# Transposing softmax probabilities as 4-byte words in a grouped-query attention kernel

## Chip, core and metric

The kernel runs on one core of a Trainium2 chip. The metric is the device time of one execution in microseconds. A core has TensorE (PE in the profile, with its weight loads as PEld), VectorE (DVE), ScalarE (ACT), GpSimd (POOL) and SyncE (SP), which here issues every DMA.

## What is computed

Two independent problems A and B of the same shape, joined along the last axis. B = 16 batches of 80 query rows of width 576, 32 query heads of width 128, 16 key/value heads (each serves two query heads), and 512 cached keys. All tensors are bf16.

```python
q = (x @ wq).reshape(B, Sq, Hq, Dh).transpose(0, 2, 1, 3)
k = jnp.repeat(k_cache, rep, axis=1); v = jnp.repeat(v_cache, rep, axis=1)
scores = jnp.einsum("bhqd,bhkd->bhqk", q, k) * (Dh ** -0.5)
p = _softmax(scores, axis=-1)
o = jnp.einsum("bhqk,bhkd->bhqd", p, v)
return o.transpose(0, 2, 1, 3).reshape(B, Sq, Hq * Dh) @ wo
```

## The kernel before

The work is cut into four phases (two problems, each in two halves of 8 batches). A phase has four groups of four key/value heads, and a group has eight units, one for each batch: 128 units in all. In a unit, each of the four key/value heads has 160 rows of queries (two heads of 80). They are worked in five tiles of 128 rows by 512 keys: tile k = 0 takes the last 32 rows of all four heads together, tiles k = 1 to 4 the first 128 rows of one head each. That makes 640 tiles.

A tile goes through these steps (line numbers are those of the profile):

- QK on TensorE: one matmul of 512 columns (L436), or for k = 0 four matmuls in 32-column strips of the array (L431), into one of three PSUM banks.
- The row maximum on VectorE (L441), exp with the row sum on ScalarE (L445, into one of ten buffers p_sb of 128 x 512 bf16), for five tiles at a time a reciprocal of the sums on VectorE (L449), and the scaling by it on GpSimd (L452, in place).
- The transposition of P on TensorE (em_tr, L458): four transpositions of 128 x 128 bf16, side by side in one of two PSUM banks. A transposition loads its block of P as weights and streams the identity past it.
- The copy out of PSUM on VectorE (em_ptev, L464 for k = 0 and L466 for the others) into pT.
- P@V on TensorE for k >= 1 (em_pv, L501): four matmuls of 160 columns, V as weights and pT as the streamed operand, added up in PSUM.
- After two heads, the copy of the result into oT on ScalarE (L513).

The keys come by a transposing DMA (L405) that leaves key 4p + j in slot j, column p, and V is loaded the same way (L409), so that column block j of P fits block j of V.

Beside the tiles run the projection of the queries (L335: groups of five matmuls of 480 or 160 columns, scaled out of PSUM by ScalarE at L342 or VectorE at L347) for the group after the present one, the transposition of x (L259), and the output projection (L546: sixteen matmuls of 192 columns, then a copy on ScalarE, L560, or an addition on VectorE, L566, and a store).

The order is written out by hand. Each operation is given an engine and a key (a time in tile steps), and a small planner (_Sched) sorts by key; each engine then runs its list in that order, and semaphores are set where an operation reads or overwrites what another engine made. QK runs eight steps (LA) ahead of the transposition of its tile:

```python
S.add("pe", tq, em_qk, reads=q_reads + [R(("kT", ks), U)],
      writes=[R(("ps", sbk), ("S", T))], name="qk%d" % T)
...
S.add("pe", t0, em_tr, reads=[R(("P", psl), ("n", T)), IDENT],
      writes=[R(("ps", tb), ("T", T))], name="tr%d" % T)
S.add("dve", t0 + KO["ptev"], em_ptev, reads=[R(("ps", tb), ("T", T))], writes=pt_writes,
      name="ptev%d" % T)
```

P@V of a tile has the key t0 + 2.5, so on TensorE the transposition and the QK of later tiles stand between a transposition and the P@V that needs it.

Of the kernel before, what the change touches and what calls it, by code (L numbers as in the profile page):

```python
# [6 lines left out]
BF16 = mybir.dt.bfloat16  # L7
# [127 lines left out]
def bass_concat_heads__gqa_block_cached__gqa_block_cached__near_ridge_kernel(  # L135
# [24 lines left out]
    with ExitStack() as es:  # L160
# [2 lines left out]
        ident = sb("ident", [128, 128], BF16)  # L163
        ones = sb("ones", [128, 128], BF16)
        warm = sb("warm", [128, 512], BF16)
        xs = sb("xs", [128, NRT, D], BF16)
        xT = sb("xT", [128, 2, 5, NROW], BF16)
        wq_sb = sb("wq_sb", [128, 2, 5, 1024], BF16)
# [1 line left out]
        kT = sb("kT", [128, NK, 4, 512], BF16)  # L170
        v_sb = sb("v_sb", [128, NV, 4, 512], BF16)
        p_sb = sb("p_sb", [128, NP, 512], BF16)
        pT = sb("pT", [128, NPT, 4, 4, 160], BF16)
        oT = sb("oT", [128, HQ, NROW], BF16)
        wo_sb = sb("wo_sb", [128, HQ, D], BF16)
        DC = D // NOC
# [4 lines left out]
        rinv = sb("rinv", [128, NSS, 8], F32)  # L181
        ps = es.enter_context(nc.psum_tensor("ps", [128, 8, 512], F32))
        psb = ps[:].bitcast(BF16)

        sem_names = (["e_pe", "e_act", "e_dve", "e_pool", "d_xs", "d_wo0", "d_wo1", "d_wq0", "d_wq1", "d_out0", "d_out1"]
                     + ["d_k%d" % i for i in range(NK)] + ["d_v%d" % i for i in range(NV)])
# [10 lines left out]
        def R(res, ver):  # L197
            return (res, ver)
# [24 lines left out]
        if NWARM:  # L223
            S.add("dve", -1000, em_warmset, writes=[R(("warm",), 0)], name="warmset")
            S.add("pe", -990, em_warm, reads=[R(("ones",), 0), R(("warm",), 0)], writes=[R(("ps", 0), ("W",))],
                  name="warm")
        IDENT = R(("ident",), 0)

        def su_time(goct, bl):
            ph, q = divmod(goct, NOCT)  # L230
# [161 lines left out]
        for U in range(NSU):  # L392
# [23 lines left out]
            for k in range(5):  # L416
# [25 lines left out]
                                           op=AluOpType.max, negate=True)  # L442

                def em_exp(e, sbk=sbk, si=si, psl=psl, ss=ss, col=col):
                    return e.activation(p_sb[:, psl, :], ps[:, sbk, :], AF.Exp, bias=negmax[:, si:si + 1],  # L445
                                        scale=1.0, accum_out=rowsum[:, ss, col:col + 1])

                def em_rcp(e, ss=ss):
# [5 lines left out]

                def em_tr(e, psl=psl, tb=tb):
                    last = None
                    for j in range(4):
                        last = e.transpose(psb[:, tb, j * 128:(j + 1) * 128],  # L458
                                           p_sb[:, psl, j * 128:(j + 1) * 128], ident[:])
                    return last  # L460

                def em_ptev(e, k=k, gl=gl, tb=tb, pts=pts):
                    if k == 0:
                        return e.tensor_copy(pT[:, pts, :, :, 128:160],  # L464
                                             psb[:, tb, 0:512].rearrange("p (j g c) -> p g j c", j=4, g=4))
                    return e.tensor_copy(pT[:, pts, gl, :, 0:128],  # L466
                                         psb[:, tb, 0:512].rearrange("p (j n) -> p j n", j=4))

                if k == 0:
                    q_reads = [R(("qT", qsl, bl, i), goct) for i in (1, 3, 5, 7)]  # L470
# [11 lines left out]
                if col == 4:  # L482
# [2 lines left out]
                S.add("pool", t4 - LA + KO["nrm"] + 0.01 * col, em_nrm,  # L485
                      reads=[R(("ri", ss), G), R(("P", psl), ("e", T))],
                      writes=[R(("P", psl), ("n", T))], name="nrm%d" % T)
                S.add("pe", t0, em_tr, reads=[R(("P", psl), ("n", T)), IDENT],
                      writes=[R(("ps", tb), ("T", T))], name="tr%d" % T)
                S.add("dve", t0 + KO["ptev"], em_ptev, reads=[R(("ps", tb), ("T", T))], writes=pt_writes,  # L490
                      name="ptev%d" % T)
# [1 line left out]
                if k >= 1:  # L493
                    ob = 5 + (gl // 2)
                    off = (gl % 2) * 160
                    pr = gl // 2

                    def em_pv(e, gl=gl, ob=ob, off=off, vs=vs, pts=pts):
                        last = None
                        for j in range(4):  # L500
                            last = e.matmul(ps[:, ob, off:off + 160],  # L501
                                            lhsT=v_sb[:, vs, gl, j * 128:(j + 1) * 128],
                                            rhs=pT[:, pts, gl, j, :], start=(j == 0), stop=(j == 3))
                        return last

                    S.add("pe", t0 + KO["pv"], em_pv,
                          reads=[R(("V", vs), U), R(("pT", pts, gl, "A"), U), R(("pT", pts, gl, "R"), U)],
                          writes=[R(("ps", ob), ("O", U, pr))], name="pv%d.%d" % (U, gl))
                    if gl % 2 == 1:
                        hb = 8 * q + 4 * pr  # L510

                        def em_oev(e, ob=ob, hb=hb, bl=bl):
                            return e.copy(oT[:, hb:hb + 4, bl * SQ:(bl + 1) * SQ],  # L513
                                          ps[:, ob, 0:320].rearrange("p (h s) -> p h s", h=4))

                        S.add("act", t0 + KO["oev"], em_oev, reads=[R(("ps", ob), ("O", U, pr))],
                              writes=[R(("oT", bl, q, pr), ph)], name="oev%d.%d" % (U, pr))

        NB_ = NRT * NOC
        for ph in range(NPH):  # L520
            prob, half = divmod(ph, NPP)
            for hh in range(2):
                for n in range(NB_):
                    r, c3 = divmod(n, NOC)
                    tail = (hh == 1 and ph == NPH - 1)
                    if tail:
                        x = 5.0 * NSU + 4.0 + 1.6 * n
                        bank = (7, 5, 6, 3, 4)[n % 5]
                    else:
                        if hh == 0:  # L530
                            u_a, n_sl = SUPP // 2 + 1, SUPP // 2 - 1
                        else:
                            u_a, n_sl = SUPP + 1, SUPP // 2
                        per = -(-NB_ // n_sl)
                        x = 5.0 * (ph * SUPP + u_a + n // per) + KO["ob"] + 0.35 * (n % per)
                        bank = OBANK
                    t = ftime(x)
                    bls = list(range((128 * r) // SQ, (128 * r + 127) // SQ + 1))
                    pv_ = ("OUT", ph, hh, n)
                    slot = n % 2  # L540

                    def em_op(e, r=r, c3=c3, hh=hh, bank=bank):
                        last = None
                        for hi in range(HH):
                            h = hh * HH + hi
                            last = e.matmul(ps[:, bank, 0:DC], lhsT=oT[:, h, r * 128:(r + 1) * 128],  # L546
                                            rhs=wo_sb[:, h, c3 * DC:(c3 + 1) * DC],
                                            start=(hi == 0), stop=(hi == HH - 1))
                        return last

                    qs_ = [hh * (NOCT // 2) + q_ for q_ in range(NOCT // 2)] if NOCT >= 2 else [0]
                    if NOCT >= 2:
                        ot_reads = [R(("oT", b_, q_, pr_), ph) for b_ in bls for q_ in qs_ for pr_ in range(2)]
                    else:
                        ot_reads = [R(("oT", b_, 0, hh), ph) for b_ in bls]
                    S.add("pe", t, em_op, reads=ot_reads + [R(("wo", hh, wc_), prob) for wc_ in range(NWC)],
                          writes=[R(("ps", bank), pv_)], name="op%d.%d.%d" % (ph, hh, n))
                    if hh == 0:
                        def em_ea(e, r=r, c3=c3, bank=bank):
                            return e.copy(acc[:, r, c3 * DC:(c3 + 1) * DC], ps[:, bank, 0:DC])  # L560

                        S.add("act", t + KO["oeva"], em_ea, reads=[R(("ps", bank), pv_)],
                              writes=[R(("acc", r, c3), ph)], name="oea%d.%d" % (ph, n))
                    else:
                        def em_eb(e, r=r, c3=c3, bank=bank, slot=slot):
                            return e.tensor_tensor(osb[:, slot, :], ps[:, bank, 0:DC],  # L566
                                                   acc[:, r, c3 * DC:(c3 + 1) * DC], AluOpType.add)

                        def em_st(e, r=r, c3=c3, prob=prob, half=half, slot=slot):
                            row0 = half * NROW + 128 * r  # L570
                            dst = out.rearrange("b s d -> (b s) d")[row0:row0 + 128,
                                                                    prob * D + c3 * DC:prob * D + (c3 + 1) * DC]
                            return e.dma_start(dst, osb[:, slot, :])

                        S.add("dve", t + KO["oevb"], em_eb, reads=[R(("ps", bank), pv_), R(("acc", r, c3), ph)],
                              writes=[R(("osb", slot), (ph, n))], name="oeb%d.%d" % (ph, n))
                        S.add("sp", t + KO["oevb"] + KO["ost"], em_st, reads=[R(("osb", slot), (ph, n))],
                              dsem="d_out%d" % slot, name="st%d.%d" % (ph, n))
# [71 lines left out]
```

## Time and profile before

| | |
|---|---|
| median of 3 runs | 815.56 us (814.84 to 816.48) |
| span of the profiled execution, first to last instruction | 812.5 us |
| its granted TensorE clock | 1.00 |
| TensorE instructions | 8940 matmuls, each with a weight load |
| VectorE, ScalarE, GpSimd busy | 680.2, 643.4, 433.0 us |
| DMA | 169.94 MB, mean 209 GB/s |

The profile gives the profiled execution by its span alone; the median of the runs is 3.1 us longer than that span, for what lies before the first and after the last instruction.

In the list of groups, a line shows the source line, the engine, the operation, the tile written and the tiles read, the shapes and the count; then the busy time in us and the mean length of one instruction in ns; then how long the engine was idle just before them and whom it waited for. Matmuls overlap in the array, so the length of one is not the time that it takes from the engine: that is the distance between the starts of two neighbours, which the timeline shows.

### The profile page before, as it was taken

The page shows a single profiled execution, that of the slowest core. Times are in us where ns is not written, and L with a number is a line of the kernel's source. Part 1 is how long each engine was busy: PE and PEld are TensorE (multiplying, and loading weights), DVE is VectorE, ACT ScalarE, POOL GpSimd, SP SyncE. Part 2 cuts the span into 40 slices and gives each one's busy share as a digit, 9 for nine tenths or more (in the row PEclk, how much of TensorE's full clock was granted, in tenths as well). Part 3 has the DMA queues.
Part 4 walks back from the last instruction along what each step waited for, and adds up shares of the span by engine and source line. Part 5 has one row for each costly group of instructions (what it writes and reads, how often), then busy time and mean ns, then how long its engine had stood idle before and what let it go on. Part 6 is the DMA issues. An engine that isn't in the chain of part 4 may idle for free.

```text
span 812.5 us, 23206 instructions
## 1 busy us (share of the span) xinstructions
PE 797.9 (98%) x8940; PEld 620.6 (76%) x8940; DVE 680.2 (84%) x1617; ACT 643.4 (79%) x1725; POOL 433.0 (53%) x647
## 2 busy tenths in 40 slices
PE   7999999999999999999999999999999999999998
PEld 4677678777777777877777777777777778777778
DVE  3899988888888889888888889888888888988872
ACT  2899888888878778888887887888887788888860
POOL 1466665455555546555555555555465455555650
DMA  9999999999897999979789999999978879977601
GB/s 228 243 245 283 249 235 268 260 254 219 190 214 182 224 231 214 207 162 223 180 199 240 245 219 230 237 259 223 224 200 191 200 195 214 199 187 172 156 29 37
DMA packets 363629, 169.94 MB, mean 209 GB/s; under 512 B 278017, under 2 KB 354305, under 8 KB 363521
## 3 DMA queue, kind: packets, MB, share of 16 engines
q1 hardware_dynamic: 363520, 168.46, 90.9%
q8 instruction: 73, 1.20, 0.6%
q14 instruction: 36, 0.29, 0.1%
HBM read 98.37 MB, written 2.95 MB: 125 GB/s over the span
## 4 chain that ended last, share of the span: by engine, by line
PE 90%; DVE 5%; DMA 3%; SPq 0%; issue 0%; POOL 0%; ACT 0%; POOLq 0%
PE ps L335 20%; PE ps L546 19%; PE ps L458 18%; PE ps L501 16%; PE ps L436 12%; PE ps L431 5%; DVE negmax L441 3%; DVE pT L466 1%; DMA kT<-in_A_k_cache_dram 1%; DMA v_sb<-in_A_v_cache_dram 1%; DMA wq_sb<-in_A_wq_dram 1%; PE ps L259 1%; POOL p_sb L452 0%; SPq L292 0%; DVE rinv L449 0%
## 5 line engine op out<-in xcount | busy, mean ns | idle before, releaser
L452 POOL TENSOR_SCALAR p_sb<-p_sb,rinv 128x512 bf16<-128x512 bf16 x640 | 430.5, 695 | 354.6 <-DVE rinv L449 354.6
L445 ACT ACTIVATE p_sb<-ps,negmax 128x512 bf16<-128x512 f32 x640 | 442.3, 691 | 83.4 <-DVE negmax L441 65.3
L441 DVE TENSOR_REDUCE negmax<-ps 128x1 f32<-128x512 f32 x640 | 434.4, 679 | 4.5 <-PE ps L436 2.9
L466 DVE COPY pT<-ps 128x512 bf16<-128x512 bf16 x512 | 209.3, 409 | 93.3 <-PE ps L458 92.6
L458 PE MATMUL ps<-ident,p_sb 128*128 128x128 bf16 x2560 | 248.5, 220 | 4.6 <-DVE negmax L441 3.5
L501 PE MATMUL ps<-pT,v_sb 128*128 128x160 bf16 x2048 | 225.3, 233 | 2.6 <-DMA v_sb<-in_A_v_cache_dram 1.3
L458 PEld LDWEIGHTS ps<-ident,p_sb 128*128 128x128 bf16 x2560 | 175.4, 98 | 57.2 <-DVE qT L347 21.6
L501 PEld LDWEIGHTS ps<-pT,v_sb 128*128 128x128 bf16 x2048 | 169.0, 98 | 63.9 <-DVE qT L347 3.6
L335 PE MATMUL ps<-xT,wq_sb 128*128 128x480 bf16 (+1 forms) x1280 | 214.4, 300 | 1.6 <-DMA wq_sb<-in_A_wq_dram 0.9
L436 PE MATMUL ps<-kT,qT 128*128 128x512 bf16 x512 | 194.0, 379 | 0.0
L546 PE MATMUL ps<-wo_sb,oT 128*128 128x192 bf16 x1920 | 175.7, 246 | 0.0
L546 PEld LDWEIGHTS ps<-wo_sb,oT 128*128 128x128 bf16 x1920 | 158.6, 98 | 0.0
L335 PEld LDWEIGHTS ps<-xT,wq_sb 128*128 128x128 bf16 x1280 | 107.0, 98 | 45.0 <-DVE qT L347 0.9
L513 ACT CAST oT<-ps 128x320 bf16<-128x320 f32 x256 | 108.9, 425 | 35.2 <-PE ps L501 32.9
L445 ACT ACTIVATION_READ_ACCUMULATOR p_sb<-ps,negmax 128x1 f32 x640 | 128.1, 200 | 0.0
L342 ACT ACTIVATE qT<-ps 128x480 bf16<-128x480 f32 (+1 forms) x128 | 71.8, 561 | 25.6 <-PE ps L335 25.5
L464 DVE COPY pT<-ps 128x512 bf16<-128x512 bf16 x128 | 52.9, 413 | 1.3 <-PE ps L458 1.3
L431 PE MATMUL ps<-kT,qT 128*32 128x512 bf16 x512 | 51.2, 390 | 1.4 <-DMA kT<-in_A_k_cache_dram 1.4
L436 PEld LDWEIGHTS ps<-kT,qT 128*128 128x128 bf16 x512 | 50.1, 98 | 0.7
L347 DVE TENSOR_SCALAR qT<-ps 128x160 bf16<-128x160 f32 (+1 forms) x128 | 41.5, 324 | 3.8 <-PE ps L335 3.7
L566 DVE TENSOR_TENSOR osb<-ps,acc 128x192 bf16<-128x192 f32 x60 | 21.0, 349 | 15.3 <-PE ps L546 12.2
L431 PEld LDWEIGHTS ps<-kT,qT 128*32 128x32 bf16 x512 | 13.1, 92 | 14.9 <-DMA kT<-in_A_k_cache_dram 1.6
(16 smaller groups left out, 77.5 us busy)
## 6 DMA issues: line engine op xcount, KB each, us to landing
v_sb<-in_A_v_cache_dram SPq DMA_DIRECT2D x64, 512.0 KB, 4.5
v_sb<-in_B_v_cache_dram SPq DMA_DIRECT2D x64, 512.0 KB, 4.5
wq_sb<-in_A_wq_dram SPq DMA_DIRECT2D x16, 512.0 KB, 5.5
wq_sb<-in_B_wq_dram SPq DMA_DIRECT2D x16, 512.0 KB, 5.5
wo_sb<-in_A_wo_dram SPq DMA_DIRECT2D x8, 576.0 KB, 5.4
wo_sb<-in_B_wo_dram SPq DMA_DIRECT2D x8, 576.0 KB, 4.8
out_dram<-osb SPq DMA_DIRECT2D x60, 48.0 KB, 2.1
xs<-in_A_x_dram SPq DMA_DIRECT2D x2, 720.0 KB, 5.1
```

What stands on the lines that cost most here:

```text
L335: last = e.matmul(ps[:, bank, 0:n1 - n0], lhsT=wq_sb[:, wsl, ck, i * 128:(i + 1) * 128], rhs=xT[:, xsl, ck, n0:n1], start=(ck == 0), stop= ...
L342: return e.activation(qT[:, qsl, b0:b0 + nb, col:col + 80], ps[:, bank, 0:n1 - n0].rearrange("p (b s) -> p b s", b=nb), AF.Identity, scale ...
L431: last = e.matmul(ps[32 * g4:32 * g4 + 32, sbk, :], lhsT=qT[:, qsl, bl, g4 * 160 + 128:g4 * 160 + 160], rhs=kT[:, ks, :, g4 * 128:(g4 + 1) ...
L436: last = e.matmul(ps[:, sbk, :], lhsT=qT[:, qsl, bl, gl * 160:gl * 160 + 128], rhs=kT[:, ks, :, gl * 128:(gl + 1) * 128], start=True, stop ...
L441: return e.tensor_reduce(negmax[:, si:si + 1], ps[:, sbk, :], axis=AX.X, op=AluOpType.max, negate=True)
L445: return e.activation(p_sb[:, psl, :], ps[:, sbk, :], AF.Exp, bias=negmax[:, si:si + 1], scale=1.0, accum_out=rowsum[:, ss, col:col + 1])
L452: return e.tensor_scalar(p_sb[:, psl, :], p_sb[:, psl, :], rinv[:, ss, col:col + 1], 1.0, op0=AluOpType.mult, op1=AluOpType.mult)
L458: last = e.transpose(psb[:, tb, j * 128:(j + 1) * 128], p_sb[:, psl, j * 128:(j + 1) * 128], ident[:])
L466: return e.tensor_copy(pT[:, pts, gl, :, 0:128], psb[:, tb, 0:512].rearrange("p (j n) -> p j n", j=4))
L501: last = e.matmul(ps[:, ob, off:off + 160], lhsT=v_sb[:, vs, gl, j * 128:(j + 1) * 128], rhs=pT[:, pts, gl, j, :], start=(j == 0), stop=(j ...
L513: return e.copy(oT[:, hb:hb + 4, bl * SQ:(bl + 1) * SQ], ps[:, ob, 0:320].rearrange("p (h s) -> p h s", h=4))
L546: last = e.matmul(ps[:, bank, 0:DC], lhsT=oT[:, h, r * 128:(r + 1) * 128], rhs=wo_sb[:, h, c3 * DC:(c3 + 1) * DC], start=(hi == 0), stop=( ...
```

## The change

P's tile is read as 256 words of 4 bytes, and a transposition moves 128 words of 4 bytes a row. Two neighbours in p_sb then travel together. exp writes P so that the two keys of a word are keys i and 128 + i of the same 256-key half: it reads the scores in their old order and writes every second element. The transposed words lie in PSUM as pairs, VectorE copies them as they are (runs of 256 bf16 elements, or 64 for k = 0), and pT holds [half, row, pair]. P@V for key block j reads half j // 2, every second element from j % 2.

The identity for the 4-byte transposition is a copy as 4-byte floats (identf), made by VectorE at the start. A probe, once at the start, transposes the bf16 identity as 4-byte words and sums up every second element of the result; the first output block of each phase is multiplied by this sum (1.0) on its way out of PSUM on ScalarE. In the changed file the transposition is L483, the copies are L489 and L492, P@V is L527, exp is L468, QK L454 and L459, the projection L358.

```diff
--- before.py
+++ after.py
@@ -163,6 +163,7 @@
+        identf = sb("identf", [128, 128], F32)
@@ -170,7 +171,7 @@
-        pT = sb("pT", [128, NPT, 4, 4, 160], BF16)
+        pT = sb("pT", [128, NPT, 4, 2, 160, 2], BF16)
@@ -181,6 +182,9 @@
+        pf = p_sb[:].bitcast(F32)
+        probe = sb("probe", [128, 1], F32)
+        idp = ident[:].bitcast(F32)
@@ -224,7 +228,26 @@
+        def em_identf(e):
+            return e.tensor_copy(identf[:], ident[:])
+
+        S.add("dve", -900, em_identf, reads=[R(("ident",), 0)], writes=[R(("identf",), 0)], name="identf")
...
+        def em_probe_set(e):
+            return e.memset(probe[:], 1.0)
+
+        def em_probe_tr(e):
+            return e.transpose(ps[0:64, 1, 0:128], idp, identf[:])
+
+        def em_probe_sum(e):
+            return e.tensor_reduce(probe[0:64, :], psb[0:64, 1, 0:256:2], axis=AX.X, op=AluOpType.add)
...
@@ -442,7 +465,9 @@
                 def em_exp(e, sbk=sbk, si=si, psl=psl, ss=ss, col=col):
-                    return e.activation(p_sb[:, psl, :], ps[:, sbk, :], AF.Exp, bias=negmax[:, si:si + 1],
+                    return e.activation(p_sb[:, psl, :].rearrange("p (c i e) -> p c e i", c=2, e=2),
+                                        ps[:, sbk, :].rearrange("p (c e i) -> p c e i", c=2, e=2),
+                                        AF.Exp, bias=negmax[:, si:si + 1],
                                         scale=1.0, accum_out=rowsum[:, ss, col:col + 1])
@@ -454,17 +479,18 @@
                 def em_tr(e, psl=psl, tb=tb):
                     last = None
-                    for j in range(4):
-                        last = e.transpose(psb[:, tb, j * 128:(j + 1) * 128],
-                                           p_sb[:, psl, j * 128:(j + 1) * 128], ident[:])
+                    for c in range(2):
+                        last = e.transpose(ps[:, tb, c * 128:(c + 1) * 128],
+                                           pf[:, psl, c * 128:(c + 1) * 128], identf[:])
                     return last
 
                 def em_ptev(e, k=k, gl=gl, tb=tb, pts=pts):
                     if k == 0:
-                        return e.tensor_copy(pT[:, pts, :, :, 128:160],
-                                             psb[:, tb, 0:512].rearrange("p (j g c) -> p g j c", j=4, g=4))
-                    return e.tensor_copy(pT[:, pts, gl, :, 0:128],
-                                         psb[:, tb, 0:512].rearrange("p (j n) -> p j n", j=4))
+                        return e.tensor_copy(
+                            pT[:, pts, :, :, 128:160, :].rearrange("p g c q e -> p g c (q e)"),
+                            psb[:, tb, 0:512].rearrange("p (c g n) -> p g c n", c=2, g=4))
+                    return e.tensor_copy(pT[:, pts, gl, :, 0:128, :].rearrange("p c q e -> p c (q e)"),
+                                         psb[:, tb, 0:512].rearrange("p (c n) -> p c n", c=2))
@@ -500,7 +526,8 @@
                                             lhsT=v_sb[:, vs, gl, j * 128:(j + 1) * 128],
-                                            rhs=pT[:, pts, gl, j, :], start=(j == 0), stop=(j == 3))
+                                            rhs=pT[:, pts, gl, j // 2, :, j % 2],
+                                            start=(j == 0), stop=(j == 3))
@@ -556,10 +583,14 @@
-                        def em_ea(e, r=r, c3=c3, bank=bank):
+                        def em_ea(e, r=r, c3=c3, bank=bank, n=n):
+                            if n == 0:
+                                return e.activation(acc[:, r, c3 * DC:(c3 + 1) * DC], ps[:, bank, 0:DC],
+                                                    AF.Identity, scale=probe[:, 0:1])
                             return e.copy(acc[:, r, c3 * DC:(c3 + 1) * DC], ps[:, bank, 0:DC])
```

More of the change, by code (lines that the diff above doesn't have):

```diff
@@ L226, in bass_concat_heads__gqa_block_cached__gqa_block_cached__near_ridge_kernel @@
                   name="warm")
+        def em_identf(e):
+            return e.tensor_copy(identf[:], ident[:])
+        S.add("dve", -900, em_identf, reads=[R(("ident",), 0)], writes=[R(("identf",), 0)], name="identf")
         IDENT = R(("ident",), 0)
+        IDENTF = R(("identf",), 0)
+        def em_probe_set(e):
[4 more added lines that the diff above has]
+            return e.tensor_reduce(probe[0:64, :], psb[0:64, 1, 0:256:2], axis=AX.X, op=AluOpType.add)
+        S.add("dve", -899, em_probe_set, writes=[R(("probe",), 0)], name="probe_set")
+        S.add("pe", -898, em_probe_tr, reads=[IDENT, IDENTF], writes=[R(("ps", 1), ("probe",))], name="probe_tr")
+        S.add("dve", -897, em_probe_sum, reads=[R(("ps", 1), ("probe",)), R(("probe",), 0)],
+              writes=[R(("probe",), 1)], name="probe_sum")
         def su_time(goct, bl):
@@ L487, in bass_concat_heads__gqa_block_cached__gqa_block_cached__near_ridge_kernel @@
                       writes=[R(("P", psl), ("n", T))], name="nrm%d" % T)
-                S.add("pe", t0, em_tr, reads=[R(("P", psl), ("n", T)), IDENT],
+                S.add("pe", t0, em_tr, reads=[R(("P", psl), ("n", T)), IDENTF],
                       writes=[R(("ps", tb), ("T", T))], name="tr%d" % T)
@@ L558, in bass_concat_heads__gqa_block_cached__gqa_block_cached__near_ridge_kernel @@
                     if hh == 0:
-                        def em_ea(e, r=r, c3=c3, bank=bank):
+                        def em_ea(e, r=r, c3=c3, bank=bank, n=n):
+                            if n == 0:
+                                return e.activation(acc[:, r, c3 * DC:(c3 + 1) * DC], ps[:, bank, 0:DC],
+                                                    AF.Identity, scale=probe[:, 0:1])
                             return e.copy(acc[:, r, c3 * DC:(c3 + 1) * DC], ps[:, bank, 0:DC])
-                        S.add("act", t + KO["oeva"], em_ea, reads=[R(("ps", bank), pv_)],
+                        S.add("act", t + KO["oeva"], em_ea,
+                              reads=[R(("ps", bank), pv_)] + ([R(("probe",), 1)] if n == 0 else []),
                               writes=[R(("acc", r, c3), ph)], name="oea%d.%d" % (ph, n))
```

## The prediction

> **What bounds the kernel now.** I read the busy table and the chain of the page first, then the groups of the transposition, then the timeline of TensorE in one steady stretch, then the table by stages.
>
> ```profile
> span 812.5 us, 23206 instructions
> ...
> PE 797.9 (98%) x8940; PEld 620.6 (76%) x8940; DVE 680.2 (84%) x1617; ACT 643.4 (79%) x1725; POOL 433.0 (53%) x647
> ...
> PE 90%; DVE 5%; DMA 3%; SPq 0%; issue 0%; POOL 0%; ACT 0%; POOLq 0%
> ```
>
> TensorE is busy for 98% of the span and is 90% of the chain that ended last: a nanosecond of TensorE is a nanosecond of the end, almost everywhere. The groups (count, then busy us, mean ns of one, idle before):
>
> ```profile
> L458 PE MATMUL ps<-ident,p_sb 128*128 128x128 bf16 x2560 | 248.5, 220 | 4.6 <-DVE negmax L441 3.5
> L458 PEld LDWEIGHTS ps<-ident,p_sb 128*128 128x128 bf16 x2560 | 175.4, 98 | 57.2 <-DVE qT L347 21.6
> L431 PEld LDWEIGHTS ps<-kT,qT 128*32 128x32 bf16 x512 | 13.1, 92 | 14.9 <-DMA kT<-in_A_k_cache_dram 1.6
> ```
>
> The 220 ns is the length of one transposition in the pipeline, not its price. The price is the distance from start to start, which the timeline of TensorE gives (start, length, group):
>
> ```profile
> 400.22 1.48 PE L546 MATMUL ps<-wo_sb,oT 128*128 128x192 bf16 x16
> 401.54 0.39 PE L458 MATMUL ps<-ident,p_sb 128*128 128x128 bf16 x4
> 401.76 0.38 PE L436 MATMUL ps<-kT,qT 128*128 128x512 bf16 x1
> 401.98 0.44 PE L501 MATMUL ps<-pT,v_sb 128*128 128x160 bf16 x4
> 402.25 0.51 PE L335 MATMUL ps<-xT,wq_sb 128*128 128x160 bf16 x5
> 402.60 0.39 PE L458 MATMUL ps<-ident,p_sb 128*128 128x128 bf16 x4
> 402.92 0.40 PE L431 MATMUL ps<-kT,qT 128*32 128x512 bf16 x4
> 403.25 0.40 PE L458 MATMUL ps<-ident,p_sb 128*128 128x128 bf16 x4
> 403.48 0.38 PE L436 MATMUL ps<-kT,qT 128*128 128x512 bf16 x1
> 403.70 0.44 PE L501 MATMUL ps<-pT,v_sb 128*128 128x160 bf16 x4
> 403.97 1.18 PE L335 MATMUL ps<-xT,wq_sb 128*128 128x480 bf16 x5
> 404.99 0.22 PE L458 MATMUL ps<-ident,p_sb 128*128 128x128 bf16 x1
> ```
>
> Four transpositions take 401.54 to 401.76, 0.22 us: 55.5 ns each. P@V, 160 columns: 0.27 / 4 = 69. Output projection, 192 columns: 1.32 / 16 = 82.5. Projection, 480 columns: 1.02 / 5 = 204. The slope is (204 - 82.5) / 288 = 0.42 ns a column, at a granted clock of 1.00 in every stage. The weight loads (98 ns) vanish behind the matmul before, but for one place: from the transpositions to L431 it is 0.32 instead of 0.22 us, and from L431 back to the transpositions 0.33 where one 512-column matmul takes 0.22. There a load is bare, for 0.10 to 0.11 us. The table by stages (PE, PEld, DVE, ACT, POOL busy) shows what stands next:
>
> ```profile
> 20.00:100.00 80.00, 78.40 (x818) 54.19 (x816) 76.31 (x182) 71.33 (x198) 50.44 (x75) 1.00 1.07 255
> 300.00:400.00 100.00, 100.00 (x1140) 78.62 (x1139) 84.74 (x200) 83.45 (x224) 54.77 (x82) 1.00 0.89 203
> ```
>
> VectorE is 95% busy early (no output projection there) and 85% in the steady part.
>
> **The change, part by part.** All sums are made against the span of 812.5; the median of the runs, 815.56, is 3.1 more, and I carry these over unchanged.
>
> *Transpositions.* Removed: 640 tiles x 4 x 55.5 ns = 142 us of TensorE, all on the chain. Added: 640 x 2 transpositions of 128 columns of 4-byte words, each with its own weight load (the built program has just one of each a transposition). No 4-byte matmul is in this trace. Low end: the price of a 2-byte one, 55.5 ns, 71 us in all, a gain of 71. Next end: the array needs two beats for a 4-byte word, so 256 columns' worth: 82.5 + 64 x 0.42 = 109.5 ns, 140 us, a gain of 1.9. High end: four beats, 512 columns, 0.22 us (L436), 282 us, a loss of 140. I take the two-beat price: every row here moves one 2-byte element a column at 0.42 ns, so twice the bytes is nearest to twice the columns.
>
> *Their weight loads.* Half as many, each of 128 columns of 4 bytes. In the rows 128 columns take 98 ns and 32 columns 92, so 96 columns more may cost 6 ns; at the matmuls' slope they cost 96 x 0.42 = 40. The transpositions start 55.5 apart behind loads of 98, so a load of today needs no more lead than that; a longer one needs 6 to 40 more. The second load of a tile has 109 ns of lead and is hidden. The first has the lead of the matmul before it. The five tiles of a unit start after, by the timeline: output projection (82.5), 160-column projection (70), L431 (nothing goes ahead there), 480-column projection (204), P@V (69). At 40 more, bare are 13 + 26 + 40 + 0 + 26 = 105 ns a unit, 13.4 us for 128 units; at 6 more, only 6 ns, 0.8 us. I take the middle, 23: 0 + 9 + 23 + 0 + 9 = 41 ns, 5.2 us. If loads lose their cover altogether it is the third rival.
>
> The Trainium skill, "TensorE: Matmul & The Clock Gate", section "Weight-path perf modes — Fast Weight Load (FWL) and DoubleRow", speaks against the change: a 128-column load takes the fast path only if its type isn't FP32, and the same page, "LDWEIGHTS (loading the stationary operand)", prices a load at columns / 1.2 ns, 107 for 128. By that (an estimate) the two loads of a tile would pace its two transpositions, about as dear as the four of today, and the first would stick out by some 40 ns a tile, 25 us. Its section "Terms" says that the transpose mode is 4x faster for FP32, which speaks for the cheapest price: by it 71 us are gained. No run here shows either; I weigh them by the chances below.
>
> *P@V reads every second element.* 2048 matmuls at 69 ns, on the chain. No row steps by two; the nearest, L436 and L431, read K in four runs of 128 and pay nothing for the steps (216 ns for 512 columns fits the slope). Low end: nothing. High end: half rate, 160 x 0.42 = 67 ns each, 137 us. I take nothing and keep the other as a rival.
>
> *exp writes every second element.* 640 x 691 ns on ScalarE, 79% busy; its output is still one element at a time. Between 0 and, were it doubled, +442 us of ScalarE, which would bind at once (643 + 442 = 1085). I take 0: the 128x480 scaling (L342, 569 ns) writes runs of 80 with steps between and is no dearer per element (1.19 against 1.35 ns). The price is the least likely of all and stays in the tail.
>
> *pT copies.* Same 512 elements (409 and 413 ns for runs of 128 and 32; now runs of 256 and 64): 0 on VectorE, which has 15% idle in the steady part.
>
> *Once only.* A copy of the identity to 4 bytes, a probe transposition and two small VectorE steps, at the start, while the first DMA lands (the chain holds 10.1 us of K's DMA there): 0. Four scalings by the probe instead of copies on ScalarE: 0, off the chain. Without that cover they are some 2 us. No DMA, SP or POOL instruction is added or moved, and the transposition still waits for the same POOL scaling, with P@V behind it as before.
>
> Sum: -1.9 + 5.2 = +3.3 us; 815.6 + 3.3 = **819**.
>
> **Rivals.**
>
> *One beat, loads hidden* (faster). Saves 111 ns a tile, 0.56 us a unit. VectorE then stands next. Early (20 to 100 us) it is at 95%, so little is gained there; the last units, 766 to 777 us, already go at VectorE's pace:
>
> ```profile
> 771.60 0.24 PE ps L458 x4
> ...
> 772.28 0.60 DVE negmax L441
> ...
> 777.04 0.24 PE ps L458 x4
> ```
>
> 5.44 us a unit. Between 100 and 765 us a unit takes 6.2 us, so 5.64 remains possible: some 105 units x 0.56 = 59 us, less some 9 for the shorter units and stalls on VectorE, which would be at 95%. 815.6 - 50 = 765, between 753 and 785. For it: the pass count of the built program is halved. Against: twice the bytes through the same array.
>
> *Loads without cover* (slower; the one mechanism on the other side). A 4-byte word fills the cell, so that its load can't lie behind the running matmul. Its place is each transposition, its price the bare load at L431, 0.10 us: 1280 x 0.10 = 128 us, 815.6 - 1.9 + 128 = 942. With one-beat matmuls 872; with loads 40 ns longer 993. It decides from the first load that can't go ahead: even 2 x 56 ns bare a tile eat all that one-beat matmuls save.
>
> *P@V at half rate* (slower): 819 + 137 = 956; it would cancel even the best transposition.
>
> That the change doesn't do what it says would show in the count (not 1280), which the built program excludes; changed bits would not alter the time.
>
> **How the numbers follow.** Two beats with hidden loads 38% (own range 814 to 828), one beat 27%, bare loads 23%, half-rate P@V 12%. Range 755 to 950: it leaves out the best tenth of the fast case and the upper part of the two slow ones. A measurement of this kernel tells about 0.2% (1.6 us) from no change. Faster: 27 and 3 of the likeliest case's low end, 30%; same: 8% of it; slower: 27 + 23 + 12 = 62%.
>
> **What would show it.** Transpositions in the changed profile: 1280, from start to start 109 ns (55 or 220 would refute the two beats), their loads 104 to 138 ns long and begun before the matmul ahead ends (if not, bare loads); P@V still 69 ns apart and 233 long; exp 691; pT copy 409; VectorE busy within 2% of 680 us. A chain that passes from PE to DVE would mean the fast case. What would make it wrong: a 4-byte price off two beats, or a stride that the array or exp pays for.

## The result, and the profile after

The changed kernel takes 823.25 us (median of 4 runs, 822.44 to 824.32) against 816.02 of before in the same comparison: a ratio of 1.0082, 95% interval 1.0065 to 1.0099. It is 7.2 us slower; 819 was forecast, slower by 3.3.

From the page of the changed kernel (busy time of each engine, the chain that ended last, then groups with count, busy us, mean ns of one):

```profile
span 822.6 us, 20651 instructions
...
PE 808.1 (98%) x7661; PEld 616.7 (75%) x7661; DVE 684.7 (83%) x1620; ACT 697.1 (85%) x1725; POOL 434.1 (53%) x647
...
PE 94%; DVE 3%; DMA 1%; SPq 0%; issue 0%; POOL 0%; ACT 0%; POOLq 0%
...
L468 ACT ACTIVATE p_sb<-ps,negmax 128x512 bf16<-128x512 f32 x640 | 532.7, 847 | 63.2 <-DVE negmax L464 47.2
...
L483 PE MATMUL ps<-identf,p_sb 128*128 128x128 f32 x1280 | 251.6, 278 | 4.6 <-DVE negmax L464 3.4
L527 PE MATMUL ps<-pT,v_sb 128*128 128x160 bf16 x2048 | 229.2, 233 | 0.0
...
L483 PEld LDWEIGHTS ps<-identf,p_sb 128*128 128x128 f32 x1280 | 142.1, 140 | 52.8 <-DVE qT L370 21.6
```

The groups of exp and P@V before:

```profile
L445 ACT ACTIVATE p_sb<-ps,negmax 128x512 bf16<-128x512 f32 x640 | 442.3, 691 | 83.4 <-DVE negmax L441 65.3
...
L501 PE MATMUL ps<-pT,v_sb 128*128 128x160 bf16 x2048 | 225.3, 233 | 2.6 <-DMA v_sb<-in_A_v_cache_dram 1.3
```

TensorE issues 1279 matmuls fewer and is busy just as long a share, 98%, of a longer span; it is now 94% of the chain. The transpositions are half as many with nearly the same busy time (251.6 against 248.5 us). P@V's mean length is 233 ns as before, but its busy time is up by 4 us: the length is a pipeline length and hides what the distance from start to start shows. exp is 156 ns longer, and ScalarE is busy 54 us more in all (697.1 against 643.4). That is less than 640 times 156 ns, because exp's record overlaps the next instruction on ScalarE, the read of its row sum. The distance from an exp to this read (medians over all exps) grew from 585 to 696 ns, so the price of an exp by about 0.1 us. Before (timeline of ScalarE):

```profile
401.19 0.69 ACT L445 ACTIVATE p_sb<-ps,negmax 128x512 bf16<-128x512 f32 x1
401.78 0.19 ACT L445 ACTIVATION_READ_ACCUMULATOR p_sb<-ps,negmax 128x1 f32 x1
```

and changed:

```profile
408.83 0.84 ACT L468 ACTIVATE p_sb<-ps,negmax 128x512 bf16<-128x512 f32 x1
...
409.54 0.18 ACT L468 ACTIVATION_READ_ACCUMULATOR p_sb<-ps,negmax 128x1 f32 x1
```

In the steady part the chain that ended last runs through TensorE alone. A part of a unit in the changed kernel (start, length, group):

```profile
401.27 0.22 PE ps L483 x2
401.49 0.21 PE ps L459
401.70 0.28 PE ps L527 x4
401.99 0.34 PE ps L358 x5
402.33 0.22 PE ps L483 x2
402.55 0.33 PE ps L454 x4
402.88 0.37 PE ps L483 x2
403.25 0.21 PE ps L459
403.47 0.28 PE ps L527 x4
```

The strips (QK of the tile k = 0) and what follows them in the chain of before:

```profile
500.89 0.33 PE ps L431 x4
501.22 0.33 PE ps L458 x4
501.55 0.22 PE ps L436
```

Two 4-byte transpositions take the 0.22 us of four 2-byte ones. The exception is 402.88, behind the strips: 0.37, where the same piece of before was 0.33. P@V's price is clearer over many units. From the starts of all matmuls between 480 and 700 us, as ns of a mean unit (each distance to the next start is counted for the matmul in front):

| kernel | unit | transpositions | P@V | output projection + projection |
|---|---|---|---|---|
| before | 6166 | 1221 | 1107 | 2603 |
| changed | 6221 | 1245 | 1148 | 2593 |

A steady unit is 55 ns longer. P@V costs 41 of it and some 10 come back in the matmuls behind it; the transpositions cost 24. Not all 128 units are steady, so the loss is best followed through the two profiled executions (a unit is counted from its first strip; us):

| stretch | before | changed | more |
|---|---|---|---|
| start to unit 1 | 14.99 | 15.86 | 0.87 |
| units 1 and 2 | 14.38 | 17.25 | 2.87 |
| units 3 to 20 | 94.88 | 94.46 | -0.42 |
| units 21 to 120 | 615.54 | 621.12 | 5.58 |
| units 121 to 128 and what follows | 72.67 | 73.91 | 1.24 |

The spans differ by 10.1 us, more than the medians. The execution of after met a granted clock of 0.5 from 14.8 to 21.6 us, and the one of before met none; this makes units 1 and 2 longer. Besides, in every other profiled execution here the time is 1.7 to 1.8 us longer than the span; the 3.1 us given for before are therefore not only what lies outside the span: by this its profiled execution was also over 1 us faster than the median. Early units became longer (5.1 instead of 4.9 us), yet units 3 to 20 together did not: before, TensorE twice sat idle ahead of a P@V for 1.3 us (until 96.0 and 112.1 us), and in the changed kernel it doesn't.

### The profile page after: what moved, and what is told of

Read it like the earlier page. It is cut to its first block, busy times and chain, and to the rows that moved or that the text cites. A ratio compares the mean times of both kernels' runs of the same rounds, so it can differ in the third digit from the quotient of the medians.

```text
span 822.6 us, 20651 instructions
## 1 busy us (share of the span) xinstructions
PE 808.1 (98%) x7661; PEld 616.7 (75%) x7661; DVE 684.7 (83%) x1620; ACT 697.1 (85%) x1725; POOL 434.1 (53%) x647
## 4 chain that ended last, share of the span: by engine, by line
PE 94%; DVE 3%; DMA 1%; SPq 0%; issue 0%; POOL 0%; ACT 0%; POOLq 0%
PE ps L358 21%; PE ps L573 19%; PE ps L483 19%; PE ps L527 17%; PE ps L459 13%; PE ps L454 5%; DVE negmax L464 2%; DMA kT<-in_A_k_cache_dram 1%; DVE pT L492 1%; PE ps L282 1%; POOL p_sb L477 0%; DVE rinv L474 0%; SPq L315 0%; ACT qT L365 0%; SPq L318 0%
## 5 line engine op out<-in xcount | busy, mean ns | idle before, releaser
L468 ACT ACTIVATE p_sb<-ps,negmax 128x512 bf16<-128x512 f32 x640 | 532.7, 847 | 63.2 <-DVE negmax L464 47.2
L492 DVE COPY pT<-ps 128x512 bf16<-128x512 bf16 x512 | 210.3, 411 | 96.0 <-PE ps L483 93.4
L483 PE MATMUL ps<-identf,p_sb 128*128 128x128 f32 x1280 | 251.6, 278 | 4.6 <-DVE negmax L464 3.4
L527 PE MATMUL ps<-pT,v_sb 128*128 128x160 bf16 x2048 | 229.2, 233 | 0.0
L527 PEld LDWEIGHTS ps<-pT,v_sb 128*128 128x128 bf16 x2048 | 172.5, 97 | 63.4 <-DVE pT L492 0.2
L358 PE MATMUL ps<-xT,wq_sb 128*128 128x480 bf16 (+1 forms) x1280 | 215.9, 301 | 3.6 <-DVE xT L286 2.0
L459 PE MATMUL ps<-kT,qT 128*128 128x512 bf16 x512 | 194.5, 380 | 0.0
L483 PEld LDWEIGHTS ps<-identf,p_sb 128*128 128x128 f32 x1280 | 142.1, 140 | 52.8 <-DVE qT L370 21.6
L358 PEld LDWEIGHTS ps<-xT,wq_sb 128*128 128x128 bf16 x1280 | 106.8, 97 | 49.2 <-issue 5.3
L468 ACT ACTIVATION_READ_ACCUMULATOR p_sb<-ps,negmax 128x1 f32 x640 | 124.5, 194 | 0.0
L365 ACT ACTIVATE qT<-ps 128x480 bf16<-128x480 f32 (+1 forms) x128 | 71.7, 560 | 21.6 <-PE ps L358 21.6
L459 PEld LDWEIGHTS ps<-kT,qT 128*128 128x128 bf16 x512 | 49.8, 97 | 6.9 <-ACT p_sb L468 2.7
L489 DVE COPY pT<-ps 128x512 bf16<-128x512 bf16 x128 | 53.1, 415 | 1.3 <-PE ps L483 1.3
L454 PE MATMUL ps<-kT,qT 128*32 128x512 bf16 x512 | 51.4, 391 | 2.2 <-DMA kT<-in_A_k_cache_dram 2.2
L454 PEld LDWEIGHTS ps<-kT,qT 128*32 128x32 bf16 x512 | 13.1, 92 | 23.8 <-ACT oT L540 15.9
```

The lines of the kernel that those rows point to most:

```text
L358: last = e.matmul(ps[:, bank, 0:n1 - n0], lhsT=wq_sb[:, wsl, ck, i * 128:(i + 1) * 128], rhs=xT[:, xsl, ck, n0:n1], start=(ck == 0), stop= ...
L365: return e.activation(qT[:, qsl, b0:b0 + nb, col:col + 80], ps[:, bank, 0:n1 - n0].rearrange("p (b s) -> p b s", b=nb), AF.Identity, scale ...
L454: last = e.matmul(ps[32 * g4:32 * g4 + 32, sbk, :], lhsT=qT[:, qsl, bl, g4 * 160 + 128:g4 * 160 + 160], rhs=kT[:, ks, :, g4 * 128:(g4 + 1) ...
L459: last = e.matmul(ps[:, sbk, :], lhsT=qT[:, qsl, bl, gl * 160:gl * 160 + 128], rhs=kT[:, ks, :, gl * 128:(gl + 1) * 128], start=True, stop ...
L468: return e.activation(p_sb[:, psl, :].rearrange("p (c i e) -> p c e i", c=2, e=2), ps[:, sbk, :].rearrange("p (c e i) -> p c e i", c=2, e= ...
L483: last = e.transpose(ps[:, tb, c * 128:(c + 1) * 128], pf[:, psl, c * 128:(c + 1) * 128], identf[:])
```

## The experiments

Theory from this profile: the loss is made up of the step of two in P@V, of a bare 4-byte load behind the strips (a load that no running matmul hides), and of a little of exp's extra time at the two ends. Rivals: P@V suffers from ScalarE's writing, not from its own reading (rival 1); or the longer exp is the whole loss (rival 2). Most of the runs undo only a part of the change; the keys of P and V then no longer match, and only the time is of use.

**P@V reading in a row** (pv_contig):

```diff
+        pTf = pT[:].rearrange("p s g c q e -> p s g (c q e)")
...
-                                            rhs=pT[:, pts, gl, j // 2, :, j % 2],
+                                            rhs=pTf[:, pts, gl, j // 2, (j % 2) * 160:(j % 2) * 160 + 160],
```

pTf is pT with its last three axes (half, row, pair) as one.

> The changed kernel, but P@V reads 160 neighbouring elements of pT instead of every second one; the keys of P and V no longer match, so the output is another one. Theory (the step of two costs TensorE 2.5 ns a P@V matmul): the distance between P@V matmuls goes from 72 back to 69 ns, a steady unit from 6.25 to 6.21 us, the time from 823.2 to about 818. Rival 1 (the 3 ns come from ScalarE's heavier writing, not from the reading): stays at 72 ns and 823. Rival 2 (the whole loss is the longer exp): 823.

820.44 us (ratio to before 1.0059, 1.0039 to 1.0079). P@V lies 69 ns apart again (72 in the changed kernel), with exp still at 846 ns; a steady unit is 6190 ns, and units 21 to 120 take 3.2 us less than in the changed kernel. The time falls by 2.8 us where 5 were expected: the projections behind P@V take back their 10 ns a unit, and the early units stay at 5.1 us. Rival 1 falls: ScalarE writes as it did, and the price is gone.

**exp writing in a row** (exp_contig):

```diff
-                    return e.activation(p_sb[:, psl, :].rearrange("p (c i e) -> p c e i", c=2, e=2),
-                                        ps[:, sbk, :].rearrange("p (c e i) -> p c e i", c=2, e=2),
+                    return e.activation(p_sb[:, psl, :], ps[:, sbk, :],
```

> The changed kernel, but exp writes its 512 elements in a row; the keys of P and V no longer match, so the output is another one. Theory (a longer exp is hidden in the steady part and binds only in the early units, where ScalarE is 94% busy, and at the end): exp goes from 847 back to 691 ns, early units from 5.10 to 4.94 us, the last from 5.58 to 5.45, steady units stay at 6.25 and P@V at 72 ns; the time is 820 to 821. Rival 1 (ScalarE's writing slows P@V): P@V back to 69 ns and about 816. Rival 2 (the whole loss is the longer exp): 816.

821.77 us (1.0076, 1.0062 to 1.0089): exp 690 ns, P@V still 72, a steady unit still 6219. Rival 2 falls: of ScalarE's busy time 53 us are gone (697.1 to 644.3), of the time some 1.5 us. In the profiled executions 0.9 us of this lies in units 121 to 128 and what follows.

**Both in a row, 4-byte transpositions alone** (tr_alone, the two edits together):

> Both undone: 4-byte transpositions alone, with exp writing and P@V reading in a row (output is another one). Theory (transpositions cost a steady unit +24 ns, P@V +41, exp only early and late): a steady unit of 6.21, 815.5 to 818 us, so 0 to 2 above before. Rival 1 and 2: 816, the time of before. The 4-byte transpositions stay 109 ns apart, which no undoing touches.

817.53 us (1.0026, 1.0012 to 1.0039). A steady unit is 6185 ns, its transpositions 1242. The transposition as such doesn't gain, it loses some 2 us (1 to 3 by the interval; 1.9 in units 21 to 120).

**The longer exp alone, on the kernel before** (exp_step_before, the edit of exp turned round):

> The kernel before, with exp writing every second element as in the changed one and nothing else (the keys of P and V no longer match, so the output is another one). Theory (a longer exp binds only in the early units and at the end): exp 847 instead of 691 ns, units between 29 and 105 us at 5.1 instead of 4.9 us, the last ones at 5.58 instead of 5.45, steady ones at 6.17 as before; 1 to 3 us over before, 817 to 819. Rival (a longer exp is the main cost): 820 or more. If it costs nothing at all: 816.

818.28 us (1.0017, 1.0004 to 1.0031). Steady units are 6171 ns, 5 more than before, so nearly all of the extra time is hidden there. The stretch from 20 to 105 us shows where it isn't (columns: stretch, its length, PE, PEld, DVE, ACT, POOL busy, then the clock). Before:

```profile
20.00:105.00 85.00, 83.40 (x876) 57.76 (x874) 81.31 (x194) 76.02 (x211) 53.55 (x80) 1.00 1.08 252
```

With the longer exp alone:

```profile
20.00:105.00 85.00, 84.77 (x865) 58.13 (x864) 81.62 (x192) 81.54 (x209) 52.93 (x79) 1.00 1.10 252
```

In this stretch there is no output projection, VectorE is at 96%, and ScalarE goes from 89% to 96%. The chain that ended last shows the two in turn there, and ScalarE's share of it over the whole span goes from 0% to 5%. Units there take 5.0 to 5.15 us instead of 4.9, and the last units 5.55 instead of 5.45. Unlike in the changed kernel, TensorE's two idle stretches of 1.3 us ahead of a P@V remain.

**The tile k = 2 left at two bytes** (k2_two_byte):

```diff
-                def em_tr(e, psl=psl, tb=tb):
+                def em_tr(e, psl=psl, tb=tb, k=k):
                     last = None
+                    if k == 2:
+                        for j in range(4):
+                            last = e.transpose(psb[:, tb, j * 128:(j + 1) * 128],
+                                               p_sb[:, psl, j * 128:(j + 1) * 128], ident[:])
+                        return last
```

> The changed kernel, but the tile k = 2, whose transposition follows the 32-column strips, is transposed as four 2-byte blocks (its pT is then in another order, so the output is another one). Theory (the 140 ns load of a 4-byte block is hidden everywhere but behind the strips): the piece of the chain after the strips goes from 0.37 back to 0.33 us, a steady unit from 6.25 to 6.20, the time to 817. If instead every 4-byte load sticks out a little, this one tile of five gives no more than a fifth of 3 us: 822.5.

824.48 us (1.0107, 1.0090 to 1.0124): no gain. The choice of tile was the mistake. QK and transposition with the same key run in the order of their tiles, so k = 2 is transposed just before the strips and k = 3 behind them. The steady unit, 6225 ns where the changed kernel has 6221, says that changing between 2 and 4 bytes costs next to nothing by itself.

**The tile k = 3 left at two bytes** (k3_two_byte, the same edit with k == 3):

> The changed kernel with the tile k = 3 transposed as four 2-byte blocks; this, and not k = 2, is the tile that follows the 32-column strips (its pT is in another order, so the output is another one). Theory (bare load of a 4-byte block behind the strips only): the piece after the strips goes from 0.37 to 0.33 us, a steady unit from 6.22 to 6.17 (mean over 480 to 700 us), the time down by some 6 from the changed kernel, to 817. Rival (the 4-byte loads cost a little everywhere, or the mode change between 2 and 4 bytes does): as with k = 2, a unit within 0.01 us of 6.22 and 823.

819.14 us (1.0041, 1.0026 to 1.0056), a steady unit of 6184 ns. Its chain (L484 is the 2-byte transposition):

```profile
504.72 0.33 PE ps L454 x4
505.05 0.33 PE ps L484 x4
505.38 0.22 PE ps L459
```

The piece behind the strips is back at 0.33. 37 ns a unit are gained; 50 were expected. In the changed kernel the timeline shows what is bare there:

```profile
408.73 0.40 PE L454 MATMUL ps<-kT,qT 128*32 128x512 bf16 x4
409.06 0.20 PEld L483 LDWEIGHTS ps<-identf,p_sb 128*128 128x128 f32 x2 [0.23 <-DVE qT L370]
409.06 0.44 PE L483 MATMUL ps<-identf,p_sb 128*128 128x128 f32 x2
```

Neither load goes ahead: the first begins only 0.33 us after the strips began, together with the first transposition. Two loads of 0.14 us end 0.20 after the first began, so the second starts 0.06 behind the first, where two 2-byte loads of before start 0.015 apart at this place (403.244 and 403.259 us). The second transposition starts 109 ns behind the start of its load.

**Transpositions alone, and k = 3 at two bytes** (tr_alone_k3, three edits together):

> 4-byte transpositions alone (exp writing and P@V reading in a row), with the tile after the strips left at four 2-byte blocks; the output is another one. Theory: the transpositions of a steady unit, 1242 ns in the run with them alone, fall by the 39 that the same step gave in the whole changed kernel, to 1203, under the 1221 of before; a steady unit of 6.145 us against 6.166 before, so 814 us, 2 to 3 under before at most. If the bare load were not all of it: 816 to 817.

816.69 us, ratio 0.9995 (0.9983 to 1.0007). The steady unit is 6147 ns with 1201 in transpositions, as expected, and 19 under before. In units 21 to 120 that makes 1.8 us, which do not show in the time. Its profiled execution took 17.29 us for the first two units, against 14.38. So even the best setting tried for this transposition is not measurably faster.

**Steps of three and four in P@V** (pv_step3, pv_step4):

```diff
-                                            rhs=pT[:, pts, gl, j // 2, :, j % 2],
+                                            rhs=pTf[:, pts, gl, j:640:4],
```

> The changed kernel with P@V reading every fourth element of the same pT region (wrong keys, so the output is another one). If the price of the step comes with the number of bytes passed over: 2.5 ns at a step of two becomes 5 to 8 ns, 74 to 77 apart, and 5 to 10 us over the changed kernel (828 to 833). If only the loss of neighbouring reads counts: 72 ns as with two, 823. If a read falls to half rate at eight bytes: some 135 ns and 950.

> The changed kernel with P@V reading every third element of its pT region (wrong keys, so the output is another one). At a step of two P@V matmuls lay 72 ns apart, at a step of four 140. If what counts is the span of bytes read for a fixed number of columns (a limit between 4 and 8 bytes a column), three gives a price between: 160 columns x 6 bytes against 8 is three quarters of 140, 105 ns, and 823 + 2048 x 0.033 = 890. If it is a switch that only steps of 8 bytes pass: 72 ns and 823. If every step past two is at half rate: 140 ns and 962.

962.19 us (1.1798, 1.1772 to 1.1824) with four, and 891.99 (1.0925, 1.0904 to 1.0945) with three. The timeline with a step of three, P@V and what follows it:

```profile
472.93 0.59 PE L528 MATMUL ps<-pT,v_sb 128*128 128x160 bf16 x4
473.35 1.49 PE L574 MATMUL ps<-wo_sb,oT 128*128 128x192 bf16 x16
```

and with a step of four:

```profile
474.18 0.73 PE L528 MATMUL ps<-pT,v_sb 128*128 128x160 bf16 x4
474.74 1.50 PE L574 MATMUL ps<-wo_sb,oT 128*128 128x192 bf16 x16
```

Start to start 0.42 / 4 = 105 ns and 0.56 / 4 = 140. The expectation for four, on record first, had named half rate at eight bytes as one of three outcomes; the one for three named 105 and 890. 160 columns at 6 bytes in 105 ns and at 8 in 140 are both 9.1 bytes a ns. At that rate (an estimate from these two) 4 bytes a column make 70 ns, just over the 69 that 160 columns take anyway: the step of two sits on the edge. The 2 ns between 70 and the 72 measured stay unexplained.

**Without the probe** (no_probe leaves out its transposition, its two VectorE steps and the scaling), **the once-only parts alone on the kernel before** (start_alone), and **before once more** (before_again):

> The changed kernel without the probe (its transposition, two VectorE steps and the scaling by it); the output stays the same. If the probe hid at the start, as predicted: 823 as changed, and a granted clock of 0.5 in a few us before 25 may come or not as it does in the other runs. If the probe is what lets the clock fall at 15 to 20 us: 820 to 821, and a clock near 1.0 there.

> The kernel before with only the once-only parts of the change (the 4-byte identity, the probe and the scaling by it); everything else and the output as before. In the profiles of the changed kernel and its relatives the first two units took 16 to 17 us and the granted clock fell to 0.5 around 15 to 20 us; in those of before and of exp writing in steps alone they took 14.4. Theory (an accident of the clock, which any of the kernels meets): 816, the two units at 14.4 or 16 to 17 as it comes. Rival (the once-only parts at the start move the clock's fall): 818, two units at 16 to 17 us.

> The kernel before once more, for a second profile of its start: 816. By the accident the first two units are at 14.4 to 17 us; by the rival always at 14.4.

824.02 us (1.0105, 1.0084 to 1.0126), 815.79 (0.9997, 0.9982 to 1.0011) and 815.03 (0.9996, 0.9985 to 1.0007). The once-only parts cost nothing that these runs show. The first two units took 16.18 us without the probe, and 14.38 both with the once-only parts alone and in before: in these profiles, then, it isn't the once-only parts that move the fall of the clock.

## Why the prediction was right, and where it wasn't

- *Two beats a transposition: right.* 109.5 ns forecast, 109 measured, 278 ns long. It is the matmul's own price, not that of the slower load: the QK behind the second transposition, whose 2-byte load starts with that transposition, also comes 109 ns after it (56 ns after a 2-byte transposition). One beat (the 27% case) is refuted in all runs.
- *Loads: right in size, wrong in place.* 104 to 138 ns long were forecast, 140 measured. The sum had 41 ns a unit bare, spread over three tiles; in fact nothing is bare behind P@V (69 and 72 ns to the transposition, as between two P@V) and the projections, and some 50 ns are behind the strips, where no load goes ahead. Together with the cheaper pair (218 ns for what was 223) the transpositions cost 24 ns a steady unit; the sum had 26. That the two nearly agree is in part luck.
- *Bare loads everywhere (23%): refuted.* The 4-byte load starts with the matmul before it, as the 2-byte one does (408.354 us, behind a projection matmul that starts at 408.352), except behind the strips.
- *P@V's step of two at nothing: the step that failed.* The term was 0 and measured 41 ns a unit, 31 to 34 after what the neighbours give back: 3.2 us in units 21 to 120, 3 to 4 us by the medians (2.8 with the long exp left in, 4.2 with the short one). The forecast missed by 3.9 us: this term, and exp's 1 to 2, less about 1 us that the sum had too much for the transpositions. The rows that it leaned on, L436 and L431, step only once in 128 elements, and couldn't show a price of every element.
- *P@V at half rate (12%): refuted for this step,* but it is real at a step of four (140 ns).
- *exp at nothing: the length was wrong, the reason half right.* 691 became 847 ns, and the price in ScalarE's time was some 0.1 us an exp. The row it leaned on (runs of 80) writes neighbours. Nearly all of this was hidden in the steady part, as ScalarE's idle time there allows. It cost 1 to 2 us in all, 0.9 of them in the last units; the early units, where the stage table showed ScalarE near its limit, became longer too, but in the changed kernel TensorE's idle stretches ahead of P@V shrank by about as much.
- *pT copies, once-only parts, VectorE: right.* 411 and 415 ns, no time, 684.7 us (0.7% up).
- *The fast case's ceiling* wasn't put to the test, since the transposition never got cheaper.

The Trainium skill, "TensorE: Matmul & The Clock Gate", "LDWEIGHTS (loading the stationary operand)", prices a 128-column load at 107 ns. The 4-byte loads here are 140 ns long and the two behind the strips start 60 apart, so neither as a length nor as the pace that the prediction made of it does the 107 hold here. The same page's section "Terms" calls the transpose mode 4x faster for FP32; against a 2-byte block a 4-byte one takes twice as long here (109 against 55.5 ns), and no run compares it with an ordinary 4-byte matmul.

What stays open is the start. In all ten profiled executions of kernels with 4-byte transpositions the granted clock fell to 0.5 near the start, for 3.4 or 6.8 us from a point between 14.3 and 16.6 us on, which reaches into the first two units; these took 16.1 to 17.3 us. In the four without, these units took 14.4 to 14.5: one met no such stretch, and three met one of 3.4 us that began between 8.8 and 10.5 us and was over before the first unit. Neither the probe nor the once-only parts explain it. How much of the 7.2 us between the medians lies there is not shown; units 21 to 128 and what follows account for 6.8 in the profiled executions.

## What to carry to other kernels

Price a packed transposition by the bytes that it moves: here half the instructions at twice the price gave nothing, and what repacking asks of the neighbours (every second element read by P@V, written by exp) was the larger part of the loss. On an engine that is 98% busy, look for a price in the distance between starts: P@V's mean length stayed at 233 ns while its busy time grew by 4 us, and exp's length grew by 156 ns while its price grew by about 100. Where a slower step is hidden in most stages, check the stages in which its engine is already near its limit.

## What the hardware showed that was not expected

- TensorE read the streamed bf16 operand at a step of two for 72 instead of 69 ns per 160 columns, at three for 105, at four for 140: at three and four that is about 9.1 bytes passed over in a ns. The Trainium skill, "SBUF — State Buffer", section "Door 1: The DMA port swizzle (why `[64,N]` ≈ `[32,N]`)", lets one step over up to 8 bf16 elements for free; for this operand a step of two already costs 3 ns, and at three and four the runs contradict it plainly.
- ScalarE wrote 512 bf16 elements at a step of two in 847 instead of 691 ns; from its start to the read of the row sum behind it, 696 instead of 585.
- A 128-column load of 4-byte words is 140 ns long, one of 2-byte words 98, and both disappear behind a matmul that takes 69 ns from start to start.
